# Fixing the program order of every engine by hand in a fused attention and long-convolution kernel, with a new setup phase

## The chip, the cores and the metric

The kernel runs on one core of one Trainium2 chip. The metric is the device time of one execution in microseconds (us). Medians and all runs are given where they matter. The engines are PE (TensorE: matmuls and transposes), DVE (VectorE), ACT (ScalarE), POOL (GpSimd) and SP (SyncE, which here only starts transfers). A run is called slow when it took over 1.5% longer than the fastest run of the same kernel; ratios use fast runs alone, while a median is of all runs of a kernel, slow ones included. The granted clock is the share of full speed that the profile says the throttle gave to PE.

## The reference, cut to what matters

```python
# four batches, 8 heads, 768 positions, head width 64; float32 in and out
scores = q @ k.T / 8 + bias          # bias falls with distance, per head
keep   = (first 8 keys) or (0 <= i - j < 96)
a      = softmax(where(keep, scores, -1e9));  x = a @ v     # heads side by side: 768 x 512
x1, x2, x3 = split(x @ w_proj)       # 512 -> 3 x 512
conv = irfft(rfft(x2) * rfft(filter))                       # along the 768 positions
out  = (x1 * conv * x3) @ w_out
```

The first eight keys ("global rows") are seen by every query. So each of seven key tiles of 128 rows holds the 8 global rows and 120 local ones. The Fourier transforms are matmuls with sine tables that the kernel makes itself. The work of a batch is attention (4 head pairs) and then the convolution.

## The kernel before: the parts that the change and the argument touch

The kernel is written as plain loops. A scheduler at build time reorders the instructions of each engine by priority and by what it thinks is ready; attention of batch b+1 is written before the convolution of batch b, so the scheduler can mix them.

```python
def load_tiles(self, dst, src, b):                 # K and V of a batch
    for t in range(7):
        g.dma_start(dst[P - (hi - lo):P, t, :, 0:D], src[b, :, lo:hi, :] ...)    # POOL starts these
        if t == 0:
            g.dma_start(dst[0:NG, 0, :, 0:D], src[b, :, 0:NG, :] ...)
    self.nc.sync.dma_start(dst[0:NG, 1:7], dst[0:NG, 0:1].to_broadcast(...))     # SP: copy global rows
# [cut]
def transposed(self, hp, qt, kt, first):
    tq = self.ps.tile([P, 1024], F16, tag="tr", bufs=1)       # one PSUM buffer for all transposes
    for st in range(6):
        nc.tensor.transpose(tq[:, P * st:P * st + P], qt[:, st, hs, :], self.ident)
    nc.vector.tensor_copy(QT, tq[:, 0:S])
# [cut: the same for K; values() also transposes through the buffer "tr"]
def run(self):
    self.constants()
    qkv = self.load_first()
    self.dft_tables(); self.load_weights(); self.masks()
    # [cut]
    self.attention(*qkv, *x, first=True)
    self.filter_spectrum(); self.inverse_tables()
    for b in range(self.B):
        if b + 1 < self.B:
            qkv = self.load_batch(b + 1)
            self.attention(*qkv, *nx)
        self.hyena(b, *x)                          # the convolution
```

The softmax here doesn't subtract the row's maximum and nothing guards it: scores larger than these inputs give would overflow.

## Time and profile before

The median was 246.4 us of three runs (242.96 to 246.85).

I cut the profile into five stages at the first projection matmul of each batch's convolution. Before the change the first projection pieces start at 54.5 us, but they flow without long gaps only from 63 us.

| stage, before | us | PE busy, us |
|---|---|---|
| setup, attention 0, filter spectrum | 54.5 | 22.4 |
| convolution 0 with attention 1 | 61.0 | 53.1 |
| convolution 1 with attention 2 | 46.5 | 43.4 |
| convolution 2 with attention 3 | 45.0 | 40.4 |
| last convolution | 36.2 | 29.5 |

The numbers come from the view of busy time by windows of the kernel before. Each line is a stretch, its length, then busy microseconds and instruction counts of PE, of PE's weight loads, of DVE, ACT and POOL, the granted TensorE clock, the DMA share and the rate:

```profile
core 0: us, PE busy (x) PEld busy (x) DVE busy (x) ACT busy (x) POOL busy (x), PEclk, DMA share, GB/s
0.00:54.50 54.50, 22.37 (x215) 12.70 (x216) 41.39 (x89) 37.03 (x46) 42.89 (x69) 0.95 2.00 189
54.50:115.50 61.00, 53.09 (x480) 31.06 (x478) 41.58 (x80) 32.31 (x52) 30.81 (x38) 0.87 1.32 97
115.50:162.00 46.50, 43.41 (x409) 24.95 (x408) 33.60 (x65) 31.22 (x52) 0.00 (x0) 1.00 0.10 36
162.00:207.00 45.00, 40.39 (x363) 22.25 (x362) 30.47 (x58) 28.76 (x48) 0.00 (x0) 1.00 0.08 30
207.00:243.20 36.20, 29.45 (x155) 14.84 (x153) 14.75 (x26) 18.54 (x35) 0.00 (x0) 1.00 0.18 69
```

PE is nearly full in the steady batches and mostly idle in the first stage. The timeline of ACT before the change shows one reason: sine and exponential tables are loaded in turn (1.28 us each), because the scheduler mixes the two uses, and the first exponential of attention (the line `E_222<-sp`) comes at 31 us. Columns are start, duration, engine, source line and operation:

```profile
27.54 1.28 ACT L234 ACT_TABLE_LOAD   x1
28.84 0.84 ACT L234 ACTIVATE fwd<-t_173 128x768 f16<-128x768 f32 x1
29.70 1.28 ACT L357 ACT_TABLE_LOAD   x1
30.99 0.89 ACT L357 ACTIVATE E_222<-sp 128x864 f16<-128x864 f32 x1
```

### The profile page before, as it was taken

How to read it: one execution, taken by the hardware profiler on the slowest of the kernel's cores; microseconds unless marked ns; L12 is line 12 of the kernel's file. 1: busy time of each engine (PE TensorE's matmuls, PEld its weight loads, DVE VectorE, ACT ScalarE, POOL GpSimd, SP SyncE). 2: the span in 40 equal slices, each digit the busy share in tenths (PEclk: the TensorE clock that was granted, in tenths of full speed). 3: DMA queues.
4: the chain of work that ended last, by engine and by line, in shares of the span. 5: the costliest groups of instructions: out<-in, count | busy, mean ns of one | idle time of the engine just before them, and what ended most of it. 6: DMA issues, size and time to landing. Idle time of an engine off the chain costs nothing.

```text
span 243.2 us, 4146 instructions
## 1 busy us (share of the span) xinstructions
PE 188.7 (78%) x1608; PEld 105.8 (43%) x1608; DVE 161.8 (67%) x314; ACT 147.9 (61%) x232; POOL 73.7 (30%) x105
## 2 busy tenths in 40 slices
PE   0221187857799958998999979899997987998963
PEld 0110123544455636654555646455554553454621
DVE  4749958798449997563778983836889543077350
ACT  3237997871368862455799625579784364672543
POOL 9768369997900399800000000000000000000000
PEclk9999997985799995999999999999999999999999
DMA  6999999999990099984200000070000002400006
GB/s 226 301 175 190 210 166 153 142 138 159 114 74 11 8 135 135 121 51 162 104 0 3 0 3 0 0 263 0 3 0 0 3 1 95 165 3 0 0 0 259
DMA packets 79627, 21.71 MB, mean 89 GB/s; under 512 B 71336, under 2 KB 76536, under 8 KB 79608
## 3 DMA queue, kind: packets, MB, share of 16 engines
q0 software_dynamic: 73584, 11.67, 71.8%
q1 hardware_dynamic: 4936, 8.21, 9.8%
q10 hardware_dynamic: 1088, 1.57, 2.1%
q8 instruction: 12, 0.20, 0.3%
q14 instruction: 7, 0.06, 0.1%
HBM read 26.48 MB, written 6.29 MB: 135 GB/s over the span
## 4 chain that ended last, share of the span: by engine, by line
PE 42%; DVE 28%; ACT 19%; DMA 5%; issue 3%; POOL 1%; ACTq 0%; POOLq 0%; DVEq 0%
PE pt L440 13%; PE pt L470 7%; PE pt L409 6%; PE pt L257 5%; DMA w<-in_moe_w_proj_dram 5%; ACT eo L458 3%; DVE xn L388 3%; ACT eo L459 3%; ACT E_225 L357 3%; PE sp L350 2%; ACT E_222 L357 2%; PE av L377 2%; DVE y L461 2%; PE tq L318 2%; DVE t_173 L227 2%
## 5 line engine op out<-in xcount | busy, mean ns | idle before, releaser
L440 PE MATMUL pt<-xT,w 128*128 128x384 f16 x256 | 46.7, 333 | 4.8 <-DVE g L445 4.8
L440 PEld LDWEIGHTS <-w 128*128 128x128 f16 x256 | 24.9, 99 | 22.8 <-issue 7.9
L318 PE MATMUL tq<-ident,qt 128*128 128x128 f16 x96 | 9.4, 236 | 24.7 <-DVE KT L332 14.9
L102 POOL DMA_DIRECT2D vt<-in_v_dram x28 | 25.1, 917 | 3.8 <-DMA w<-in_moe_w_proj_dram 2.7
L470 PE MATMUL pt<-wo,y 128*128 128x512 f16 x96 | 22.1, 379 | 4.3 <-DVE y L464 4.3
L357 ACT ACTIVATE E_222<-sp 128x864 f16<-128x864 f32 x24 | 21.5, 897 | 6.0 <-PE sp L350 3.0
L357 ACT ACTIVATE E_225<-sp 128x864 f16<-128x864 f32 x24 | 21.4, 893 | 4.5 <-PE sp L350 3.8
L114 POOL DMA_DIRECT2D qt<-in_q_dram x18 | 16.3, 926 | 19.2 <-PE sp L350 15.6
L350 PE MATMUL sp<-QT,KT 64*128 64x216 f16 (+2 forms) x224 | 18.9, 254 | 4.1 <-ACT E_222 L357 2.0
L473 ACT ACTIVATE t<-pt 128x512 f32<-128x512 f32 x24 | 13.5, 598 | 11.4 <-PE pt L470 11.4
L393 ACT COPY xT<-tx 128x768 f16<-128x768 f16 x16 | 12.8, 803 | 12.0 <-PE tx L392 11.9
L102 POOL DMA_DIRECT2D kt<-in_k_dram x21 | 18.9, 940 | 1.5 <-DMA w<-in_moe_w_proj_dram 1.2
L318 PEld LDWEIGHTS <-qt 128*128 128x128 f16 x96 | 7.0, 105 | 27.6 <-DVE KT L332 15.4
L456 PE MATMUL pt<-inv,X 128*128 128x384 f16 x96 | 16.9, 326 | 2.3 <-ACT eo L458 2.3
L257 PE MATMUL pt<-dst,fwd 128*128 128x512 f16 x72 | 18.5, 380 | 0.0
L411 ACT CAST dst<-pt 128x512 f16<-128x512 f32 x24 | 13.9, 586 | 6.8 <-PE pt L409 6.7
L388 DVE TENSOR_TENSOR xn<-av,rc 128x896 f16<-128x896 f32 x16 | 17.3, 1084 | 0.2
L350 PEld LDWEIGHTS <-KT 64*128 64x128 f16 x224 | 8.8, 96 | 17.2 <-issue 13.0
L409 PE MATMUL pt<-w,xa 128*128 128x512 f16 x48 | 15.4, 429 | 0.9 <-DVE h_576 L290 0.9
L470 PEld LDWEIGHTS <-y 128*128 128x128 f16 x96 | 9.0, 98 | 15.7 <-DVE y L464 5.7
L417 ACT CAST X<-pt 128x512 f16<-128x512 f32 x24 | 14.0, 587 | 2.1 <-PE pt L257 1.4
L456 PEld LDWEIGHTS <-X 128*128 128x128 f16 x96 | 9.4, 98 | 8.8 <-issue 3.0
(218 smaller groups left out, 379.0 us busy)
## 6 DMA issues: line engine op xcount, KB each, us to landing
out_dram<-t SPq DMA_DIRECT2D x24, 256.0 KB, 2.2
vt<-in_v_dram POOLq DMA_DIRECT2D x24, 128.0 KB, 5.8
qt<-in_q_dram POOLq DMA_DIRECT2D x18, 128.0 KB, 5.7
kt<-in_k_dram POOLq DMA_DIRECT2D x18, 128.0 KB, 5.5
t<-in_k_dram ACTq DMA_DIRECT2D x4, 384.0 KB, 7.2
t<-in_q_dram SPq DMA_DIRECT2D x4, 384.0 KB
w<-in_moe_w_proj_dram POOLq DMA_DIRECT2D x3, 512.0 KB, 11.6
fl<-in_moe_filter_fft_dram POOLq DMA_DIRECT2D x1, 768.0 KB, 9.6
```

Source lines behind the costliest of these rows:

```text
L102: g.dma_start(dst[P - (hi - lo):P, t, :, 0:D], src[b, :, lo:hi, :].rearrange("h p d -> p h d"))
L114: g.dma_start(qt[:, t], self.q[b, :, P * t:P * t + P, :].rearrange("h p d -> p h d"))
L257: self.nc.tensor.matmul(pt, self.fwd[:, kt, s, :], src[:, kt, :], start=(kt == 0), stop=(kt == 2))
L318: nc.tensor.transpose(tq[:, P * st:P * st + P], qt[:, st, hs, :], self.ident)
L350: nc.tensor.matmul(sp[:, hh, off:off + w], KT[64 * hh:64 * hh + 64, o:o + P], QT[64 * hh:64 * hh + 64, KL * m:KL * m + w], start=(off == 0 ...
L357: nc.scalar.activation(eo, sp[:, :, 0:432].rearrange("p h (m w) -> p h m w", m=2), Act.Exp, scale=self.scale)
L388: nc.vector.tensor_mul(xn, ov[:, :, :, 0:D], rc.to_broadcast([P, 7, 2, D]))
L409: nc.tensor.matmul(pt, src[:, c, P * t:P * t + P], self.w[:, c, DM:2 * DM], start=(c == 0), stop=(c == 3))
L417: nc.scalar.copy(X[:, s], pt)
L440: nc.tensor.matmul(pt[:, 0:h], self.w[:, c, o + P * j:o + P * j + P], xT[:, c, h * s:h * s + h], start=(c == 0), stop=(c == 3))
L456: nc.tensor.matmul(pt[:, 0:h], X[:, s, cs], self.inv[:, s, :], start=(s == slots[0]), stop=(s == slots[-1]))
L470: nc.tensor.matmul(pt, y[:, c, P * t:P * t + P], self.wo[:, c, :], start=(c == 0), stop=(c == 3))
```

## The change

Its intent is to spend PE's idle time. It does four things:

1. Everything is emitted inside a block that fixes the written order on all five engines; the scheduler no longer reorders.
2. Attention and convolution are cut into pieces, and a weave emits them alternately by planned fractions; some DVE work is put off by a piece ("after").
3. The sine angles are made by one-row matmuls (outer products), with fewer DVE and POOL steps; the filter's two halves are added on POOL; filter spectrum and inverse tables move from setup into batch 0.
4. Empty matmuls on zeros are put into the setup phase and into attention 0.

```diff
     def run(self):
-        nc = self.nc
-        self.constants()
-        qkv = self.load_first()
-        self.dft_tables()
-        self.load_weights()
-        self.masks()
+        engines = mybir.EngineType
+        with self.tc.manual_schedule(engines={engines.PE, engines.Activation, engines.DVE,
+                                              engines.Pool, engines.SP}):
+            self.emit()
+
+    def emit(self):
[cut: constants]
+        ths = [self.dft_angles(a) for a in range(4)]
+        self.busy(10)
[cut]
+        self.weave((self.attention(*qkv, *x, first=cast), 33, 0, 1))
         for b in range(self.B):
+            streams = [(self.hyena(b, *x), 30, 0, 1)]
             nx = None
+            if b == 0:
+                streams.insert(0, (self.filter_stage(), 9, 0.05, 0.3))
             if b + 1 < self.B:
                 qkv = self.load_batch(b + 1)
+                if b == 0:
+                    self.load_w_out()
                 nx = self.new_x()
-                self.attention(*qkv, *nx)
-            self.hyena(b, *x)
+                streams.insert(0, (self.attention(*qkv, *nx), 33, 0.25 if b == 0 else 0.0, 0.9))
+            self.weave(*streams)
             x = nx
[cut: attention as a list of pieces]
         for i in range(n + 1):
+            for live, fn in ((i < n, lambda: sc(i, 0)),
+                             (i + 2 < n and first, lambda: cast(i + 2)),
+                             (i > 0, lambda: val(i - 1, 0)),
+                             (i + 1 < n, lambda: trk(i + 1)),
+                             (i < n, lambda: sc(i, 1)),
+                             (i > 0, lambda: val(i - 1, 1)),
+                             (i + 1 < n, lambda: trq(i + 1)),
+                             (i < n, lambda: sc(i, 2)),
+                             (i > 0, lambda: trx(i - 1))):
+                if live:
+                    fn()
+                    if first:
+                        self.busy(1)
+                    yield 1
[cut: the convolution yields after each piece; the eight gates are spread between its matmuls]
+    def busy(self, n):
+        if n:
+            pt = self.mm()
+            for _ in range(n):
+                self.nc.tensor.matmul(pt, self.idle[:, 0:P], self.idle, start=True, stop=True)
```

A gate is a tile of x1 times x3: eight projection matmuls, ACT's copy of x1 and DVE's product. Here `sc` is a group of scores, `val` the value products of one head, `trk`, `trq` and `trx` the transposes of K, Q and the normalised values, all three through the one PSUM buffer "tr" (`bufs=1`).

## The prediction

> **What bounds it now.** The page shows a span of 243.2 us, PE busy 78%, DVE 67%, ACT 61%. The chain of waits and the table by windows cut it into stages:
> - 0 to 62.8 us: setup, attention 0, filter spectrum. PE is busy for only 28 us here. The chain runs through DVE and ACT: angle tables on DVE from 18.8 us, Sin and Exp tables loaded in turn (eight loads, 1283 ns each), the first exponential only at 31.0 us.
> - 62.8 to 114.9: convolution 0 with attention 1, 52.1 us, granted clock 0.90.
> - 114.9 to 161.3 and 161.3 to 207.2: 46.4 and 45.9 us. From starts in the timeline, convolution needs 29.2 us of PE (24 projections 5.2, 18 DFT 3.9, 64 gates 10.7, 24 inverse 4.0, 24 output 5.4) and attention 12.2 us (80 transposes at 0.07, scores 3.5, 104 value products at 0.031). Sum 41.4, so 4.7 us per batch are waits: attention is spent early, then the gates wait for DVE (1.56 + 0.55) and inverse and output for evacuations (0.75, 1.33).
> - 207.2 to 243.2: last convolution alone, 36.0 us.
>
> **What the change does.**
> Setup: DVE's angle products (about 8 us) become one-row matmuls plus four ACT copies; DVE constants shrink; Sin and Exp are loaded about once each; filter halves go to POOL; POOL builds masks before its loads. In program order I estimate the angle folds done at 10 us, the sines at 12.7, table load and two masks at 15.5, first exponential at 16.5 instead of 31. From there attention 0 is DVE's: 28 us of DVE work from the trace's durations (Q/K copies and casts 11.8, mask products 7.8, reciprocal and normalise 6.4, butterflies 2.2), 24 left at the first exponential. With dependency gaps, the first projection matmul comes at about 47 us (43 to 52) instead of 63.4.
> The filter spectrum moves into batch 0: PE 46.6 us ideal, DVE about 42; I estimate 50 (before 52.1).
> Steady batches: the weave keeps the work and spreads it. It should recover most of 4.7 us, but SyncE is in program order too: the copy of K's global rows for batches 2 and 3 stands behind the last output store, and the K transposes need it. Evacuation 0.6, two issues of 0.7 and a landing of about 2 us, against 1.5 us of other PE work, cost about 2.5 us per boundary. I estimate 44.5 each.
> Last batch: gates fill the inverse's gaps, but the last gate now precedes the output; 35 us.
>
> [...] They take about 2 us per head pair where PE has slack.
>
> **Sum.** 47 + 50 + 2 x 44.5 + 35 = 221 us of span, against 243.2; runs are about 2.5 us longer: 223.5 us, range 213 to 236. Faster by over 2%: 0.91; within 2%: 0.06; slower: 0.03.
>
> **What would show it.** First exponential near 16.5 us; two or three table loads; first projection near 47; clock near 1.0 after 15 us; steady period 43 to 46; K transposes waiting for the K copy at 97 and 142 us.
>
> **What would make it wrong.** In-order engines stalling each other, most in batch 0, where DVE is nearly full; late loads (POOL waits for the filter before loading batch 1); slow POOL additions; attention 0 bound by latency, not DVE (first projection above 52).

A passage on the empty matmuls is cut from the record: it claimed an effect of theirs on the clock that no trace or run of this case shows. "They", in the sentence left of that paragraph, are these matmuls. The sum came to 47 + 50 + 2 x 44.5 + 35 = 221 us of span and 223.5 us for a run. The 2.5 us between the two were an estimate; the traced run of the kernel before has 1.9 (245.12 us against a span of 243.2).

## More of the kernel before

The timeline of SP's transfer queue before the change, around the end of the first convolution, shows that the scheduler put the copy of K's global rows for batch 2 (`kt<-kt`) ahead of the six output stores of batch 0:

```profile
98.80 0.69 SPq L107 DMA_DIRECT2D kt<-kt  x1
107.47 0.69 SPq L107 DMA_DIRECT2D vt<-vt  x1
112.11 3.79 SPq L474 DMA_DIRECT2D out_dram<-t  x6
```

## The result and the profile after

The changed kernel took 254.44 us median (253.55 to 254.71, four runs, all fast), the kernel before 244.68 us on the same chips: a ratio of 1.049, 95% interval 1.0446 to 1.0534. It is slower by 5%, where I had given 3% to that. Two of the four runs of the kernel before (246.4 and 246.85 us) count as slow beside 242.44, so few runs carry this ratio; against the medians of the later rounds (244.4 to 245.8 us) the change is about 4% slower. All ratios here are the mean time of one kernel's fast runs over that of the other's fast runs of the same rounds, so not quite the ratio of the medians that I quote.

The same windows view of the changed kernel, cut at the same events:

```profile
core 0: us, PE busy (x) PEld busy (x) DVE busy (x) ACT busy (x) POOL busy (x), PEclk, DMA share, GB/s
0.00:50.20 50.20, 35.33 (x298) 18.28 (x299) 33.41 (x79) 28.45 (x38) 37.90 (x52) 0.86 1.44 170
50.20:110.30 60.10, 48.72 (x437) 26.89 (x436) 42.19 (x85) 36.56 (x61) 26.43 (x33) 1.00 1.19 80
110.30:165.80 55.50, 44.32 (x398) 24.06 (x396) 33.57 (x71) 29.88 (x51) 14.07 (x17) 0.91 0.98 79
165.80:213.80 48.00, 41.97 (x391) 23.12 (x389) 33.58 (x71) 29.61 (x50) 0.00 (x0) 1.00 0.10 34
213.80:252.70 38.90, 31.11 (x155) 15.33 (x153) 14.71 (x27) 18.75 (x35) 0.00 (x0) 0.96 0.17 61
```

The first two stages together end 5 us earlier than before (110.3 against 115.5 us). The three later ones are 9.0, 3.0 and 2.7 us longer. PE is busy only 0.9 to 1.7 us longer in them than before; the rest is waiting.

The setup did what was meant. In ACT's timeline after the change the sines are one run, one table load follows, and the first exponential starts at 15 us instead of 31:

```profile
8.41 2.40 ACT L261 ACTIVATE fwd<-th 128x512 f16<-128x512 f32 x4
10.82 1.28 ACT L202 ACT_TABLE_LOAD   x1
12.12 1.38 ACT L202 ACTIVATE mask<-dm 128x648 f16<-128x648 f32 x2
13.40 0.81 ACT L140 CAST t<-t 128x768 f16<-128x768 f32 x1
14.97 0.89 ACT L478 ACTIVATE E_96<-sp 128x864 f16<-128x864 f32 x1 [0.76 <-PE sp L471]
```

Where PE waited shows in the table of waits of the changed kernel, PE alone: who waited on which line, for what, total us, times, longest.

```profile
PE tk L459 <- DMA kt<-kt: 11.3, 2, 8.2
PE o L498 <- DMA vt<-vt: 5.8, 1, 5.8
PE tx L515 <- DVE QT L439: 5.7, 6, 1.4
PE pt L602 <- DVE X L568: 3.0, 3, 2.2
```

The two largest are the on-chip copies of global rows. SP's timeline after the change says why. The copy for batch 2 now stands behind the six stores of batch 0, because its loads are written after that batch's convolution (the dots stand for two copies for batch 1):

```profile
20.70 0.88 SPq L110 DMA_DIRECT2D vt<-vt  x1
...
103.78 7.36 SPq L624 DMA_DIRECT2D out_dram<-t  x6
111.43 1.36 SPq L110 DMA_DIRECT2D kt<-kt  x1
113.10 1.37 SPq L110 DMA_DIRECT2D vt<-vt  x1
160.92 5.71 SPq L624 DMA_DIRECT2D out_dram<-t  x6
166.93 0.71 SPq L110 DMA_DIRECT2D kt<-kt  x1
```

In PE's timeline at that place the transposes of K (`tk`) stop after the first of seven, and PE, which must keep the fixed order, does nothing for 8.22 us although projection matmuls stand right behind:

```profile
111.18 0.22 PE L459 MATMUL tk<-ident,kt 128*128 128x128 f16 x1
119.62 0.80 PE L459 MATMUL tk<-ident,kt 128*128 128x128 f16 x6 [8.22 <-DMA kt<-kt]
120.21 1.06 PE L532 MATMUL pt<-w,xa 128*128 128x512 f16 x2
```

Two theories were open. Theory A: the late copies are the loss. Theory B: the fixed order is slow in itself, and the copies only take the place of other waits.

### The profile page after: what moved, and what is told of

It is laid out like the page before. It is cut to its first block, busy times and chain, and to the rows that moved or that the text cites. A ratio compares the mean times of both kernels' runs of the same rounds, so it can differ in the third digit from the quotient of the medians.

```text
span 252.7 us, 4276 instructions
## 1 busy us (share of the span) xinstructions
PE 201.4 (80%) x1670; PEld 107.7 (43%) x1670; DVE 157.5 (62%) x333; ACT 143.2 (57%) x233; POOL 78.4 (31%) x100
## 3 DMA queue, kind: packets, MB, share of 16 engines
q0 software_dynamic: 73584, 11.67, 70.9%
q1 hardware_dynamic: 6024, 9.79, 11.6%
## 4 chain that ended last, share of the span: by engine, by line
PE 31%; DVE 26%; POOL 15%; DMA 15%; ACT 6%; issue 5%; SPq 0%; POOLq 0%; DVEq 0%; ACTq 0%
PE pt L620 7%; PE pt L532 6%; DVE g L550 5%; PE pt L545 5%; POOL vt L105 5%; DMA fl<-in_moe_filter_fft_dram 5%; DMA kt<-kt 4%; DMA qt<-in_q_dram 3%; PE pt L316 3%; POOL kt L105 3%; DVE xn L508 3%; PE tx L515 2%; DMA kt<-in_k_dram 2%; POOL qt L117 2%; PE pt L602 2%
## 5 line engine op out<-in xcount | busy, mean ns | idle before, releaser
L545 PE MATMUL pt<-xT,w 128*128 128x384 f16 x256 | 47.9, 332 | 0.5 <-ACT dst L534 0.4
L545 PEld LDWEIGHTS <-w 128*128 128x128 f16 x256 | 23.8, 99 | 17.6 <-issue 4.2
L478 ACT ACTIVATE E_99<-sp 128x864 f16<-128x864 f32 x24 | 21.5, 898 | 12.4 <-PE sp L471 11.9
L602 PE MATMUL pt<-inv,X 128*128 128x384 f16 x96 | 19.5, 334 | 3.8 <-DVE X L568 3.0
L269 PE MATMUL pt<-idle 128*128 128x512 f16 x44 | 20.0, 511 | 1.2 <-DVE idle L645 1.2
L508 DVE TENSOR_TENSOR xn<-o,rc 128x448 f16<-128x448 f32 x32 | 20.0, 624 | 1.1
L515 PE MATMUL tx<-ident,xn 128*128 128x128 f16 x112 | 8.9, 219 | 11.6 <-DVE QT L439 5.7
L460 DVE COPY KT<-tk 128x896 f16<-128x896 f16 x12 | 7.4, 619 | 14.4 <-PE tk L459 14.4
L459 PE MATMUL tk<-ident,kt 128*128 128x128 f16 x84 | 7.3, 225 | 11.3 <-DMA kt<-kt 11.3
L471 PEld LDWEIGHTS <-KT 64*128 64x128 f16 x224 | 7.5, 95 | 19.2 <-issue 15.4
L604 ACT CAST eo<-pt 128x384 f16<-128x384 f32 x16 | 7.7, 484 | 12.7 <-PE pt L602 6.8
```

The costliest lines, as they stand in the source:

```text
L269: self.nc.tensor.matmul(pt, self.idle[:, 0:P], self.idle, start=True, stop=True)
L471: nc.tensor.matmul(sp[:, hh, off:off + w], KT[64 * hh:64 * hh + 64, o:o + P], QT[64 * hh:64 * hh + 64, KL * m:KL * m + w], start=(off == 0 ...
L478: nc.scalar.activation(eo, sp[:, :, 0:432].rearrange("p h (m w) -> p h m w", m=2), Act.Exp, scale=self.scale)
L508: nc.vector.tensor_mul(xn[:, :, hh, :], o[:, :, 0:D], rc.to_broadcast([P, 7, D]))
L545: nc.tensor.matmul(pt[:, 0:h], self.w[:, c, o + P * j:o + P * j + P], xT[:, c, h * s:h * s + h], start=(c == 0), stop=(c == 3))
L602: nc.tensor.matmul(pt[:, 0:h], X[:, s, cs], self.inv[:, s, :], start=(s == slots[0]), stop=(s == slots[-1]))
```

## The experiments

Seventeen kernels ran, all correct; each had four runs (one of them profiled) beside seven of the kernel before. Stage lengths are read from the profile of each, cut at the first projection matmul of each batch. Runs r1, r11 and r13 had their profile in a slow run, so no stage length of theirs is used. The medians of r1, r3, r11, r13, r15 and r16 have one or two slow runs in them; the ratios have none. "Free" means that the scheduler may reorder that engine when the program is built; the others keep the written order.

| run | median us | ratio to before | stages, us |
|---|---|---|---|
| before | 244 to 246 | 1 | 54.5, 61.0, 46.5, 45.0, 36.2 |
| the change | 254.44 | 1.049 | 50.2, 60.1, 55.5, 48.0, 38.9 |
| r1 no copies | 242.32 | 0.982 | |
| r2 copies a batch ahead | 239.40 | 0.979 | 50.5, 60.1, 45.2, 44.8, 37.2 |
| r3 nothing fixed | 224.74 | 0.917 | 47.9, 56.5, 42.6, 42.3, 33.9 |
| r4 no empty matmuls | 257.09 | 1.050 | 50.5, 62.1, 55.8, 50.9, 37.2 |
| r5 POOL, SP free | 241.06 | 0.988 | 52.2, 60.1, 45.2, 44.8, 37.2 |
| r6 r2, DVE free | 237.86 | 0.976 | 53.1, 58.9, 44.1, 43.7, 34.9 |
| r7 r2, PE free | 235.68 | 0.968 | 45.9, 64.4, 44.0, 44.0, 36.1 |
| r8 r2, ACT free | 244.54 | 1.003 | 54.3, 59.3, 45.2, 44.8, 38.9 |
| r9 r2, PE and DVE free | 226.98 | 0.931 | 47.4, 58.0, 42.7, 42.4, 34.0 |
| r10 r2, ACT and DVE free | 236.75 | 0.971 | 53.4, 58.1, 44.1, 43.7, 34.9 |
| r11 r2, PE, DVE, ACT free | 223.28 | 0.911 | |
| r12 r3 without the weave | 228.88 | 0.939 | 48.8, 55.7, 44.0, 43.9, 34.0 |
| r13 V's memset later | 255.58 | 1.041 | |
| r14 r2, two pieces moved | 240.64 | 0.986 | 49.4, 60.4, 45.8, 45.4, 37.4 |
| r15 r14, PE, DVE, ACT free | 223.91 | 0.907 | 47.4, 54.3, 42.3, 41.9, 33.9 |
| r16 batch 3 loaded later | 249.86 | none | 51.1, 60.1, 49.6, 49.6, 37.2 |
| r17 r3, no empty matmuls | 224.76 | 0.913 | 46.7, 54.8, 42.6, 42.3, 34.0 |

### r1 and r2: take the late copies away

r1 loads the global rows from DRAM into every tile, so there is no copy:

```diff
         for t in range(7):
-            lo = max(0, self.K0[t] - NG)
-            hi = self.K0[t] + KL
-            g.dma_start(dst[P - (hi - lo):P, t, :, 0:D], ...)
-            if t == 0:
-                g.dma_start(dst[0:NG, 0, :, 0:D], src[b, :, 0:NG, :]...)
-        self.nc.sync.dma_start(dst[0:NG, 1:7], dst[0:NG, 0:1].to_broadcast(...))
+            lo, hi = self.K0[t], self.K0[t] + KL
+            g.dma_start(dst[NG:P, t, :, 0:D], src[b, :, lo:hi, :]...)
+            g.dma_start(dst[0:NG, t, :, 0:D], src[b, :, 0:NG, :]...)
```

> The eight global rows of K and V are loaded from DRAM into every tile by small loads of POOL, and the three kinds of on-chip copies on SyncE are gone (POOL issues 6 small loads more per tensor, about 3.5 us of its time). Theory A (late copies): the profile of the change shows PE waiting 6.0 us for the V copy in setup, 8.4 us and 3.1 us for the K copy at the two batch boundaries, so 254.4 falls by 13 to 18 us, to 237 to 241, and no K transpose waits over 1 us at a boundary. Theory B (the fixed order itself is slow, the copies only take the place of waits that come anyway): it falls by under 6 us, to 248 or more, and the same time shows up as waits for DVE and ACT.

r2 keeps the copies but writes each batch's loads one batch earlier, so that SP meets them before the previous stores:

```diff
             if b + 1 < self.B:
-                qkv = self.load_batch(b + 1)
                 if b == 0:
+                    loaded = [self.load_batch(1)]
                     self.load_w_out()
+                if b + 2 < self.B:
+                    loaded.append(self.load_batch(b + 2))
+                qkv = loaded.pop(0)
```

> Loads and copies stay, but each batch's are issued one batch ahead, so that SyncE meets the copies before the previous batch's stores. Theory A: the two boundary waits (8.4 + 3.1 us) go, the setup wait of 6.0 us stays: 254.4 minus about 11, so 242 to 245. Theory B: over 249.

r1 took 242.32 us median; two of its four runs were slow, and its fast ones took 241.30 and 239.67 us, the one just above and the other inside A's range. No transpose of K waits for a copy in its (slow) profile, but PE still waits 4.9 us for V in the setup, which I had expected to go. r2 took 239.40 us, 2.6 us under A's range. Its SP timeline has the copy for batch 2 ahead of the stores:

```profile
71.88 0.69 SPq L110 DMA_DIRECT2D kt<-kt  x1
79.65 0.69 SPq L110 DMA_DIRECT2D vt<-vt  x1
104.10 7.36 SPq L624 DMA_DIRECT2D out_dram<-t  x6
125.29 0.71 SPq L110 DMA_DIRECT2D kt<-kt  x1
```

The two steady stages fell from 55.5 and 48.0 to 45.2 and 44.8 us:

```profile
110.60:155.80 45.20, 42.24 (x399) 23.53 (x397) 33.48 (x71) 29.79 (x51) 14.08 (x17) 1.00 1.18 97
155.80:200.60 44.80, 41.85 (x392) 23.14 (x390) 33.57 (x71) 29.58 (x50) 0.00 (x0) 1.00 0.09 34
```

So the late copies cost 13.5 us, 10.3 and 3.2 in these two stages. The medians differ by 15.0 (254.4 against 239.4); the rest lies in the last stage. That stage, 38.9 in the change's profile and 37.2 in r2, has no copy in it: the granted clock was 0.96 in the one and 1.00 in the other, and r16, which keeps the late copies, has 37.2 too. I take that difference for the run's, not the copies'.

### r3 and r5: free the engines

r3 takes the block away that fixes the order. r5 fixes PE, ACT and DVE but leaves POOL and SP free.

```diff
-        with self.tc.manual_schedule(engines={engines.PE, engines.Activation, engines.DVE,
-                                              engines.Pool, engines.SP}):
-            self.emit()
+        self.emit()                                                        # r3
+        with self.tc.manual_schedule(engines={engines.PE, engines.Activation, engines.DVE}):   # r5
```

> The same program, emitted in the same woven order, but the scheduler may reorder each engine again. Theory A: the compiled order shows one of the two K copies still behind no store and all copies ahead of the first stores, so the boundary waits go: 240 to 248. Theory B: the scheduler repairs in-order stalls as well and comes below r1, under 237.

> The changed kernel with PE, ACT and DVE fixed by hand as before, POOL and SyncE free for the scheduler. If the cost of fixing splits into a SyncE/POOL part (copies behind stores) and a compute part, this is the compute part alone: 237 to 242, like r2. If the two parts are one thing, it comes near r3 (225) or stays at 254.

r3 took 224.74 us. Both theories hold a part: with the order free, the same program is 8% faster than the kernel before. Its windows:

```profile
0.00:47.90 47.90, 32.60 (x249) 17.11 (x249) 31.60 (x68) 28.85 (x37) 34.31 (x49) 0.88 1.60 171
47.90:104.40 56.50, 53.54 (x486) 29.63 (x487) 45.30 (x97) 38.62 (x65) 40.10 (x50) 0.95 2.19 112
104.40:147.00 42.60, 41.73 (x399) 23.38 (x395) 32.75 (x71) 29.68 (x51) 3.47 (x4) 1.00 0.49 79
147.00:189.30 42.30, 41.43 (x392) 23.10 (x390) 32.74 (x71) 29.54 (x50) 0.00 (x0) 1.00 0.10 36
189.30:223.20 33.90, 29.39 (x155) 14.72 (x153) 14.45 (x27) 18.57 (x35) 0.00 (x0) 1.00 0.19 69
```

In a steady stage PE is now busy for 41.4 of 42.3 us; in r2 it was 41.85 of 44.8. So it idles 0.9 us instead of 3.0.

r5 took 241.06 us, as expected, so the cost of fixing has two separate parts: 13 to 15 us from SP and POOL (r2 and r5 agree on it), and about 14.7 us more from PE, ACT and DVE (r2 less r3). By stages, r2 less r3, the second part is 2.6, 3.6, 2.6, 2.5 and 3.3 us: it lies everywhere. The stages of r2 and r5 differ in the setup alone (50.5 and 52.2 us).

### r4 and r17: no empty matmuls

```diff
     def busy(self, n):
-        if n:
+        if False:
             pt = self.mm()
```

> All 44 empty matmuls taken out. They take 9.5 us of PE at full clock in the first 50 us, where PE waits anyway. If they hold the clock as meant: setup gets slower by 1 to 3 us without them (granted clock under 0.7 in the first 50 us). If they only fill the queue: 0 to 2 us faster. I expect within 2 us of 254.4.

> r3 (nothing fixed, 224.7) without the empty matmuls. By hand they were worth 2.6 us (r4, 257.1 against 254.4). Under the scheduler setup has fewer long waits, so I expect 0 to 3 us slower: 225 to 228. Under 224: they cost more than they give.

r4 took 257.09 us. That is 2.7 us above the median of the change, but the ratios to the kernel before of the same rounds are 1.050 and 1.049, so I read no difference; I had reckoned with 2.6 us when I wrote what I expected of r17. r17 took 224.76 us (0.913) against r3's 224.74 (0.917): no difference either. Whatever the empty matmuls do to the time is below what these runs can show, about 2 us either way.

### r6 to r11: which engine's order is it?

All start from r2 and free one or more engines; r8 and r10 are the same edit with other names.

```diff
-        with self.tc.manual_schedule(engines={engines.PE, engines.Activation, engines.DVE,
-                                              engines.Pool, engines.SP}):
+        with self.tc.manual_schedule(engines={engines.PE, engines.Activation,
+                                              engines.Pool, engines.SP}):    # r6: DVE free
```

> r2 (copies early, 239.4) with DVE alone freed. Theory C1: DVE's fixed order puts the copies out of the one transpose bank behind pieces that are not ready, and PE waits (transposes of x for QT, inverse for X): most of the 14.7 us between r2 and r3 returns, 226 to 232. Theory C2 (PE's own fixed order is what costs): 236 to 240.

> r2 with PE alone freed. Theory C1: PE has other matmuls to take but DVE's pieces still come in the fixed order: 234 to 240. Theory C2: 225 to 231.

> r2 with ACT alone freed. Both theories: ACT is busy 60% and few PE waits name it, so 237 to 241. Under 235 would say that ACT's order (filter evacuations, eo copies) is a third cause.

r6 took 237.86, r7 235.68, r8 244.54 us. So C1 and C2 both fall: freeing DVE alone returns 1.5 us of 14.7 (its ratio, 0.976, is not clear of r2's 0.979), PE alone 3.7, and freeing ACT alone is 5 us worse, which I had not expected. The record shows where: its steady stages are those of r2, but its setup is 3.8 us longer, and its last stage, 1.7 us longer, ran at a granted clock of 0.96. With ACT free the scheduler put a mask before the sines, so there are four table loads instead of two, and the first exponential comes at 20.9 us instead of 14.8. What remained was that the orders are coupled:

> r2 with PE and DVE freed together, ACT, POOL and SyncE by hand. r6 and r7 freed one each and got back 1.6 and 3.7 of the 14.7 us between r2 and r3. Theory D (the fixed orders are coupled: each waits for another that is fixed, so freeing one finds no ready work): much more than the sum of 5.3, that is 222 to 230. Rival (each engine's order has its own cost): 233 to 236, the sum.

> r2 with ACT and DVE freed, PE, POOL and SyncE by hand. If PE's woven order is good and only the evacuations are in the wrong order: 225 to 231. If PE's order is part of the coupling: 234 to 240.

> PE, ACT and DVE all free, POOL and SyncE by hand with the copies a batch ahead. All of r3's gain should be here: 221 to 227; the V loads stand ahead of the weights as by hand, so setup may be up to 3 us shorter than r3's 47.9.

r9 took 226.98 us: PE and DVE together return 12.4 us, where the two alone summed to 5.3. That is what theory D expected. r10 took 236.75: with PE still fixed, freeing ACT and DVE returns only 2.7. r11, with only POOL and SP by hand, took 223.28 us median with one slow run in it (256.97 at a clock of 0.755); its fast runs took 220.82 to 223.98, so all of the second part is back.

The stages say where the excess over the sum lies. In the last three stages the returns simply add: 4.5 us for DVE (r6), 3.1 for PE (r7), 8.1 for both (r9). Setup and batch 0 together do not: 110.6 us in r2, 112.0 in r6, 110.3 in r7 and 105.4 in r9. One reason: in r3 and in every one of these runs with DVE or ACT free (r6, r8, r9, r10) the scheduler put the sines later, and the first exponential came at 20.5 to 23.1 us, against 14.8 in r2. In r6 this goes with a setup 2.6 us longer, which hides part of what DVE returns later. And r7's batch 0 ran at a granted clock of 0.92 against 1.00 in r2, so part of its 64.4 us may be clock. So theory D is shown for the total, not for the steady batches, where by one profile each the rival fits: each engine's order has its own cost. No run kept the hand order for the setup alone.

How a stall can spread is shown in part: in the 8.22 us stop above, PE took none of the projection matmuls that stood behind the transposes of K. With every order fixed, a piece that is late on DVE holds up PE (in the change the transposes `tx` waited six times for DVE's copy of Q, 5.7 us in all), and the PE work that DVE's next pieces need is then late as well. This last link is argued; what is shown are these waits and the times and stages above.

### r14: a better hand order?

If a few named places were at fault, moving them should help. r14 is r2 with `trx` one piece later, and with three gates instead of one between the last batch's DFT and its inverse:

```diff
-        for i in range(n + 1):
+        for i in range(n + 2):
             for live, fn in ((i < n, lambda: sc(i, 0)),
+                             (i > 1, lambda: trx(i - 2)),
[cut]
-                             (i < n, lambda: sc(i, 2)),
-                             (i > 0, lambda: trx(i - 1))):
+                             (i < n, lambda: sc(i, 2))):
[cut: in the convolution of the last batch]
+        last = b == self.B - 1
+        for _ in range(2 * last):
+            gate(*next(gates))
+            yield 1
```

> r2 (all by hand, copies early) with two pieces moved in the order: the transposes of the normalised values come one piece later, after the next scores, and in the last batch three gates instead of one stand between the DFT and the inverse. Theory: in r2's steady batches PE waits mostly where these transposes meet DVE still busy with the piece before (QT copy 1.85 us, xn 0.6 of 4.4 us), and in the last batch where the inverse meets the spectrum products (2.3 us). So steady batches fall from 45.0 to 43 to 44 and the last from 37.2 to 34.5 to 36, the time from 239.4 to 234 to 237. If the waits only move to another piece: 238 to 240.

It took 240.64 us, with steady stages of 45.8 and 45.4 and a last one of 37.4. The expectation of a gain is a miss; the waits moved. (The last stage ran at a granted clock of 0.95, against 1.00 in r2: PE was busy there for 30.7 us against 29.4, and idle for 6.6 against 7.8. So about 1.2 us of waiting did go there, and the longer PE time hid it.) PE's longest waits in r2, from 115 to 200 us:

```profile
PE tx L515 <- DVE QT L439: 3.1, 4, 0.8
PE o L498 <- DVE E L490: 0.9, 2, 0.4
PE tx L515 <- DVE xn L508: 0.8, 2, 0.4
```

and in r14, same stretch:

```profile
PE sp L471 <- ACT E L478: 2.1, 2, 1.1
PE sp L471 <- ACT X L571: 1.7, 2, 0.8
PE tx L515 <- DVE xn L508: 1.7, 2, 0.8
```

The wait of the transposes for DVE's copy of Q is gone, as meant. In its place the scores (`sp`) wait for ACT. Two moves do not prove that no good hand order exists; they show that removing the largest named wait did not shorten the steady stage.

### r12: what is the weave worth when the order is free?

```diff
     def weave(self, *streams):
+        if len(streams) > 1:
+            ... run each stream to its end, filter first, convolution last
+            return
```

> r3 (nothing fixed) without the weave: attention, filter and convolution are emitted one after the other as in the kernel before, the new setup and the empty matmuls stay. If r3's 20 us against before come from setup alone, this is 225 to 229; if the woven emission is worth the 4 us a steady batch that the stages suggest (46.5 to 42.6, and 2 in the last), this is 232 to 238.

It took 228.88 us, at the upper end of the first expectation (225 to 229) and well under the second: the weave is worth about 4 us (steady stages 44.0 and 43.9 against 42.6 and 42.3), and the other 15 us of r3's gain come without it, from the rest of the change. I did not divide those further, except that r17 shows no effect of the empty matmuls.

### r13 and r16: why 8.2 us at one boundary and 3.1 at the other?

At the first boundary POOL's loads of batch 3 were on their way; at the second nothing was being loaded. r13 was to move those loads earlier by moving V's memset behind the loads of Q and K:

```diff
         self.load_tiles(kt, self.k, b)
+        self.nc.gpsimd.memset(vt[:, :, :, self.D:self.D + 1], 1.0)
         self.load_tiles(vt, self.v, b)
```

> The changed kernel, all engines by hand, copies still behind the stores; only the memset of V's ones column is moved behind the loads of q and k on POOL, so that batch 3's q and k are loaded when their buffers come free (about 75 to 90 us) and not at 105 us, when attention 1 gives V's buffer back. Theory: the first boundary's K copy waited 8.2 us because 3 us were queue order (as at the second boundary, where nothing was loading) and 5 us were those loads on the same DMA engines. Then this boundary's wait falls to 3 to 4 us and the time to 248 to 250. If the traffic does not matter, the wait stays 8 us and the time 254.

It did not do that. The loads started at 93 us instead of 105, since Q's buffer was not free earlier (POOL waited 15.7 us for PE's scores), and V's were still being issued until 114. The time stayed (255.58 us). r13 tells nothing about the traffic.

r16 holds the loads back instead:

```diff
+                if b == 2:
+                    held = self.sp.tile([1, 2], F16, bufs=1)
+                    nc.gpsimd.tensor_copy(held, self.probe[0:1, 2, 0:2])    # convolution 1's half
                 qkv = self.load_batch(b + 1)
```

> The changed kernel, all engines by hand, copies behind the stores. POOL copies two elements of convolution 1's second projected half before it loads batch 3, so these loads start near 125 us and no longer overlap the K copy at 111 us (r13 failed to bring that about: its loads only moved to 93 to 114). Theory: queue order costs about 3 us and the loads on the same DMA engines the other 5 of the first boundary: its wait falls from 8.4 to about 3 us, PE's clock does not drop, and the time falls to 247 to 250. If traffic does not matter: wait 8 us, 254.

Now the loads start at 124.5 us, and PE's waits of r16 between 100 and 125 us have this line in place of 8.2:

```profile
PE tk L459 <- DMA kt<-kt: 3.0, 1, 3.0
```

The time was 249.34 and 246.50 us in its two fast runs (the other two, 252.43 and 250.38, count as slow), too few for an interval, but 5 to 8 us below the change. So, by this one profile, about 3 us of the first wait are queue order and about 5 went with the loads that were moving at the same time: 8.2 us with them against 3.0 without. The page of the change counts POOL's queue and SP's as shares of the same 16 DMA engines (70.9% and 11.6%); how the copy lost its 5 us there is not shown. The V copy of the setup (5.8 us of waiting) was also issued while weights were loading; no run took that traffic away.

### r15: the version that the experiments point to

Loads a batch ahead, POOL and SP by hand, PE, DVE and ACT free, and r14's two moves.

> The same two moves with PE, ACT and DVE left to the scheduler and only POOL and SyncE by hand, as r11 (223.3). The scheduler already fills these waits, so the moves should give little: 220 to 224.

It took 223.91 us, 0.907 of the kernel before (interval 0.9027 to 0.9110); its fast runs took 221.59 and 222.62 us, and the other two, 225.21 and 225.38, count as slow. r11, without the two moves, is within the noise of it. Both beat both kernels.

## Why the prediction was wrong, point by point

| stage | predicted | the change | order free (r3) |
|---|---|---|---|
| setup and attention 0 | 47 | 50.2 | 47.9 |
| batch 0 | 50 | 60.1 | 56.5 |
| batch 1 | 44.5 | 55.5 | 42.6 |
| batch 2 | 44.5 | 48.0 | 42.3 |
| last | 35 | 38.9 | 33.9 |

The predicted total was the time of the same program with the order free (223.5 against 224.74), and not that of the program as it was built. That is partly luck: r3 has no late copies, for which I had planned 5 us, and ends setup and batch 0 7.4 us later than predicted but the other three stages 5.2 us earlier.

1. **"The weave keeps the work and spreads it. It should recover most of 4.7 us" is the step that failed.** I costed each stage from the work on each engine, with a small loss for the order: 44.5 us less the 2.5 for the copy is 42.0. With PE and DVE both fixed, a steady batch without the copy waits took 45.2 and 44.8 us (r2), PE idle for 3.0 of them; with both free it took 42.7 and 42.4 (r9), PE idle for 0.9. In the fixed order nothing takes the place of a matmul that has to wait; the scheduler had ordered the work so that fewer had to. Over all stages the fixed compute orders cost 14.6 us (r2 less r3). I named "in-order engines stalling each other" among what would make the prediction wrong, but gave it no microseconds.
2. **"Cost about 2.5 us per boundary" had the right mechanism and the wrong size.** K's copy stood behind the last store, the transposes of K waited for it, and at the first boundary that was 8.2 us (granted clock 0.91 in that stage), at the second 3.1. I had not seen that POOL would load batch 3 at that moment, because V's buffer comes free only then (at 105.2 us; POOL had waited 30.4 us for it); r16 shows that this makes the difference.
3. **"I estimate 50" for batch 0 was mis-sized.** It took 60.1 us. PE was busy for 48.7 of them, where I had 46.6, and idle for 11.4, where I had 3.4: sixteen waits, most of them on DVE and ACT and one on a load of K (0.65 us), none over 1.6 us. I had rated the DVE and ACT work of filter and attention as hidden. The 56.5 us of r3 are not the same work: there 49 matmuls of attention 0 run after the first projection (486 in the stage against 437), and PE idles for only 3.0 us. Taken together, setup and batch 0 end at 104.4 us in r3, 7.4 us after the predicted 97; so about that much of the miss is not the fixed order, and to which wait it is due stays open.
4. **Setup was close.** The first exponential came at 15.0 us (predicted 16.5) with two table loads, as predicted (the trace before has seven, not the eight of the prediction). The first projection came at 50.2, inside my 43 to 52. I missed that V's copy would hold up PE for 5.8 us.
5. **"35 us" for the last batch** came out at 38.9, and 37.2 in r2. With PE and DVE free it was 34.0 (r9).
6. **The empty matmuls** were put in to hold the clock. That they do was my assumption, and it is not shown: leaving them out changed neither program by more than the noise (r4, r17), and with them the clock was not the "near 1.0 after 15 us" of the prediction. It was 0.74 from 20 to 40 us; over the first stage it was 0.86 with them and 0.92 without (r4), 0.88 and 1.00 with the order free (r3, r17). The trace before does not tie the recorded clock to PE's work either: PE did nothing from 20 to 28 us, yet the clock is recorded at 1.00 until 39 us, while from 50 to 60 us, with PE busy for 7.6 of 10 us, it is 0.66.

The misses add up: 3.2 + 10.1 + 11.0 + 3.5 + 3.9 = 31.7 us over the predicted 221 us of span, which is the 252.7 us of the profile. By the stages, 14.6 of them are the fixed compute orders (r2 less r3), 8.5 the late copies beyond the 5 us planned, 1.7 the last stage (PE busy for 31.1 us at a recorded clock of 0.96, against 29.4 at 1.00 in r2), and the remaining 6.9 the estimates themselves, mostly those of setup and batch 0.

Two things stay open. Whether the hand-made setup with a free order after it would be faster still was not tried. And whether a hand order exists that matches the scheduler was tried in two moves only.

## What to carry to other kernels

Before you fix an engine's order by hand, list for each queue what will stand behind what, the transfer queues first: here a 48 KB copy written behind six stores started at 111.4 us, and at 71.9 us when it was written ahead of them (r2). With two engines that feed each other, one fixed order can keep most of the loss: of the 12.4 us that PE and DVE returned together, 10.9 stayed when only DVE was freed and 8.7 when only PE was. So build the same program with engines freed one by one and in pairs, and compare stage by stage, before you trust the hand order. A stage's work per engine gives a floor, not a time (batch 2 of r2 had 41.9 us of PE work and took 44.8); give "in-order stalls" its own term.

## What else these traces show

- What a small copy loses beside other loads: PE waited 8.2 us for a 48 KB copy beside the loads of a batch, and 3.0 us without them (r16).
- Matmuls that contradict the recorded clock: the profile grants a clock of 1.00 from 0 to 10 us of the change, yet the empty 128x512 matmuls there start 0.43 us apart (their weight loads below), while the 24 projections of the same size from 213.83 to 219.01 us, also at 1.00, take 0.216 us each.

```profile
7.28 0.15 PEld L269 LDWEIGHTS <-idle 128*128 128x128 f16 x1 [0.28 <-issue]
7.71 0.15 PEld L269 LDWEIGHTS <-idle 128*128 128x128 f16 x1 [0.28 <-issue]
8.13 0.15 PEld L269 LDWEIGHTS <-idle 128*128 128x128 f16 x1 [0.28 <-issue]
```

- What fixed orders on several engines cost together: freeing DVE returned 1.5 us, PE 3.7, both 12.4 (r6, r7, r9).
- POOL against DVE: an addition of 128x1536 two-byte values took 3.09 us on POOL after the change (POOL's spans are rough), and 0.94 us on DVE before it, a third.
